# Moving the end of the wide steps, the decay broadcasts and the output stores in a gated-attention plus feed-forward kernel

## Chip, cores and metric

The kernel runs on one core of a Trainium2 chip. The metric is the device time of one execution in microseconds (us). Before the change the median of three runs is 555.83 us (551.5 to 556.11).

## What is computed

For 4 batches and 8 heads of width 40, a recurrence over 768 positions keeps a 40x40 matrix `C`, a vector `n` and a running maximum `m` for each head:

```
m_new = max(f + m, i);  f_stab = exp(f + m - m_new);  i_stab = exp(i - m_new)
C = f_stab * C + i_stab * v k^T;   n = f_stab * n + i_stab * k
y = sigmoid(o) * (C q) / max(|n.q|, 1)
```

The 3072 tokens of 320 features that come out go through a feed-forward layer: `h = x @ w_in` (320x2048), `g = softplus(h)`, `out = g @ w_out` (2048x320). All is float32.

## The kernel before, in words

The recurrence is worked out in chunks of 128 positions: one **step** `s` is one batch and one chunk with all 8 heads, 24 steps in all. Three steps (`g` = 0, 1, 2) make a **tile** of 384 tokens, and there are 8 tiles `t`. The feed-forward layer of a tile is `products()` (L881): for each of 16 slices of `w_in`, 8 matmuls into `hp` (L929), and two slices later 9 matmuls into `po` (L900). These 17 matmuls per slice, 272 per tile, are the **products**, and their running count `n` is the clock by which all other work is placed: after each product `tick(n)` (L865) runs every generator whose place has come. A place only fixes the order of instructions on each engine and on each DMA queue; an instruction then runs when its semaphores allow it, so a queue that has nothing to wait for runs ahead of the products.

Each value of the layer is kept as a high and a low part: `gh` and `ab` on ScalarE (ACT, L806 and L808), `gl` on GpSimd (POOL, L811). `hp` has three buffers, and the `po` products run two slices behind, so these three have some slices' time.

The steps of tile `t` are placed in the products of tile `t`-1. The six tiles from 2 on are **wide** (feature-major). A wide step has a base, in products, and its parts stand at offsets from that base (L257 to L260, `wide_step` L760): its load (L345: six copies of q and k between buffers, sometimes three of a parked state, and the values `vt`, all issued by SyncE, SP) at -48 (or -45 for g = 0); the broadcast read of the decays `fb` (`decays`, L404, SP) at -22; the two scans that make `pw` of them (L413, VectorE, DVE) at 4, then `gw` (L434) and on POOL `vw` (L440); scores `sp` at 6 and 14; the state update `cp` on TensorE (PE, L461), which reads `vw`, at 31; the copies of the new state `cn` (L472, L473, SP) at 53; the products with the old state `iq` at 50 and 62, each followed by a DVE product into `y` (L540); the values `yq` (L548) at 68. Then `y` is turned round through DRAM by DMAs that ACT issues: written at 79 (`yd`, L560), read back at 107 (`read_wide` L562: `yx`, and last the normalizer `nw`, L568). `finish_wide` (L570: four DVE instructions, the first on `nw`) stands at 119 plus a distance `d`, and `end_wide` (L578) at 139 plus `d`: a DVE product, a copy on ACT three products later and a DVE subtraction (L586) three products after that give `X`, the input of the tile's products. `d` is NEAR = 18 for tile 2 and AWAY = 44 for the later ones (L789). The bases of a tile's three steps are some 91 products apart; for g = 2 of tile t > 2 the base is 272t - 200.

The products of tile `t` begin at count 272t - 18. There `products` (L915) first runs all that is queued until the tile's three steps are emitted.

`prepare(t)` (L266) loads q and k of a tile (`loq`, `lok`), splits them on ACT (`hiq`, `hik`) and POOL; the load copies from these. `wide_gates` (L327) loads the output gates of three tiles at a time into `eg` (SP) at `GP`, and applies the sigmoid on ACT 30 products later. When a tile's `po` is complete, `result` (L943) copies it to `ob`, two of three parts on ACT and one on DVE, and stores it four products later through SP. The first two tiles use another, plain form (`plain_step`, L712).

Of the kernel before, what the change touches and what calls it, by code (L numbers as in the profile page):

```python
# [17 lines left out]
NG = 3  # L18
# [14 lines left out]
WIDE = 2  # L33
# [6 lines left out]
def mlstm_moe_kernel(  # L40
# [10 lines left out]
    nc = tc.nc  # L51
# [194 lines left out]
    def weights_out(u):  # L246
# [9 lines left out]

    (W_LOAD, W_FB, W_SCAN, W_CN, W_CS, W_VW, W_SP0, W_SP1, W_Y, W_CP, W_CD,  # L257
     W_IQ0, W_IQ1, W_VI, W_YQ, W_YD, W_RD, W_NM, W_FIN) = (
        -48, -22, 4, 19, -6, 4, 6, 14, 17, 31, 47, 50, 62, 38, 68, 79, 107, 119, 139,
    )  # L260
    N_LOAD, N_FB, N_SCAN, N_CN, N_VW, N_SIG, N_SP0, N_SP1, N_CP, N_CD, N_IP, N_VI, N_YP, N_X, N_XP = (
        -35, -22, 25, 5, 8, 18, 11, 27, 46, 46, 45, 46, 56, 72, 68,
# [76 lines left out]
        yield GL  # L339

    GL = 30
    GP = [150, 1088]
    eg = {}

    def load(z):  # L345
        t, n, gs = z.t, z.n, slice(z.g * D, (z.g + 1) * D)
        if t < PLAIN:

            k = 128 if z.s < 3 else D
            room, tags = (p1, ("loq", "lok")) if z.s == 2 else (p2, ("qst", "kst"))  # L350
            z.qst = room.tile([k, H, L], F32, tag=tags[0], name=f"qst{n}")
            z.kst = room.tile([k, H, L], F32, tag=tags[1], name=f"kst{n}")
            if k > D:
                with tc.issue_after(eye.ins):
                    (nc.gpsimd if z.s == 2 else nc.vector).memset(z.qst, 0.0)
                    nc.gpsimd.memset(z.kst, 0.0)
            nc.sync.dma_start(z.qst[0:D], qk[t, 0, gs])
            nc.sync.dma_start(z.kst[0:D], qk[t, 1, gs])
        else:
            (qh, ql), (kh, kl) = parts[t]  # L360
            z.qst = p2.tile([D3, H, L], F32R, tag="qst", name=f"qst{n}")
            z.kst = p2.tile([D3, H, L], F32R, tag="kst", name=f"kst{n}")
            for r, (a, e) in enumerate(((qh, kh), (qh, kl), (ql, kh))):
                nc.sync.dma_start(z.qst[r * D : (r + 1) * D].bitcast(F32), a[gs].bitcast(F32))
                nc.sync.dma_start(z.kst[r * D : (r + 1) * D].bitcast(F32), e[gs].bitcast(F32))
        if t > 0:
            z.old = None
            if z.c > 0 and not stays(z.b, z.c - 1):
                z.old = p2.tile([D3, H, E2], F32, tag="cn", name=f"pk{n}")
                for r in range(3 if t >= PLAIN else 1):  # L370
                    nc.sync.dma_start(z.old[r * D : (r + 1) * D], park[z.b])
        if z.s != NG:
            load_values(z)
# [16 lines left out]
    def decays(z):  # L390

        z.fbs = []
        h0 = z.b * H
        for i in range(2):
            if z.s < 2:
                fb = ps_h.tile([128, HG, L], F32, tag="hp", name=f"fb{z.n}_{i}")
                for j in range(HG):
                    h = h0 + i * HG + j
                    nc.tensor.matmul(
                        fb[:, j, :], ident[:, h : h + 1].broadcast_to([128, 128]), fg0, start=True, stop=True  # L400
                    )
            else:
                fb = p2.tile([128, HG, L], F32, tag="fb", name=f"fb{z.n}_{i}")
                nc.sync.dma_start(fb, fz_d[z.c, h0 + i * HG : h0 + (i + 1) * HG, :].partition_broadcast(128))  # L404
            z.fbs.append(fb)

    def decay(z):

        z.pws = []
        for i, fb in enumerate(z.fbs):  # L410
            pw = p2.tile([128, HG, L], F32, tag="pw", bufs=4, name=f"pw{z.n}_{i}")
            flat = "p h t -> p (h t)"
            nc.vector.tensor_tensor_scan(  # L413
                pw.rearrange(flat), fb.rearrange(flat), ident4.rearrange(flat), 0.0, ALU.mult, ALU.add
            )
            z.pws.append(pw)
# [19 lines left out]
    def state_values(z):  # L436

        z.vw = work(z, p1, "vw", [128, H, E], "vw", p1, ("vw", "vi", "yy")[z.s % NG])
        v1 = z.v1.rearrange("p (h e) -> p h e", e=E)
        nc.gpsimd.tensor_tensor(z.vw, v1, z.gw.broadcast_to([128, H, E]), op=ALU.mult)  # L440
# [22 lines left out]
    def new_state(z):  # L463
        s, cn = z.s, z.cn
        if z.c > 0:
            nc.vector.tensor_tensor(cn[0:D, :, 0:E], cn[0:D, :, 0:E], z.cp, op=ALU.add)
        else:
            nc.scalar.copy(cn[0:D, :, 0:E], z.cp)
        yield
        if stays(z.b, z.c):  # L470
            if ORDER.index((z.b, z.c + 1)) >= PLAIN * NG:
                nc.sync.dma_start(cn[D : 2 * D], cn[0:D])  # L472
                nc.sync.dma_start(cn[2 * D : D3], cn[0:D])  # L473
            Cst[z.b] = cn
        else:
            nc.sync.dma_start(park[z.b], cn[0:D])
        yield
# [64 lines left out]
    def values_wide(z):  # L542

        yq = ps_a.tile([PP + EP, HG, L], F32, tag="pa", name=f"yq{z.n}")
        for h in range(H):
            p, i = divmod(h, 2)
            e0, e1 = i * PP, PP + i * EP
            nc.tensor.matmul(  # L548
                yq[e0:e1, p, :], z.via[:, h * E : h * E + e1 - e0], z.pws[h // HG][:, h % HG, :], start=True, stop=True
            )  # L550
        yield YQD
        if z.c > 0:
            nc.vector.tensor_tensor(z.y, yq, z.y, op=ALU.add)  # L553
        else:
            nc.vector.tensor_copy(z.y, yq)
        yield "write"
        z.yd = dpool.tile([EP * H, L], F32, tag="yd", bufs=2, name=f"yd{z.n}")
        rows = z.yd.rearrange("(d p i) t -> i d p t", p=HG, i=2)
        for i in range(2):
            nc.scalar.dma_start(rows[i], z.y[i * PP : i * PP + EP])  # L560
# [199 lines left out]
    def wide_step(z):  # L760
        yield W_LOAD if z.g else -45
        load(z)
        yield W_FB
        decays(z)
        yield W_SCAN
        decay(z)
        last = z.c == NC - 1
        yw = values_wide(z)

        def y():  # L770
            for r in yw:
                if r == "write":
                    return
                yield r

        c = new_state(z)
        ev = [(W_Y, lambda: load_decays(z))]
        if not last:
            ev += [(W_CN, lambda: old_state(z)), (W_VW, lambda: last_decays(z)), (W_VW, lambda: state_values(z))]
        if z.c > 0:  # L780
            ev += [(W_CS, lambda: stack(z))]
        ev += [(W_SP0, lambda: scores(z, 0)), (W_SP1, lambda: scores(z, 1))]
        if not last:
            ev += [(W_CP, lambda: state(z)), (W_CP + 6, lambda: next(c)), (W_CD + 6, lambda: next(c))]
        if z.c > 0:
            ev += [(W_IQ0, lambda: inter_wide(z, 0)), (W_IQ1, lambda: inter_wide(z, 1))]
        ev += [(W_VI, lambda: gate_values(z)), (W_YQ, y), (W_YD, lambda: next(yw, None)), (W_RD, lambda: read_wide(z))]

        d = AWAY if z.t > WIDE else NEAR  # L789
        ev += [(W_NM + d, lambda: finish_wide(z)), (W_FIN + d, lambda: end_wide(z))]  # L790
        ev.sort(key=lambda e: e[0])
        for w, f in ev:
            yield w
            r = f()
            if hasattr(r, "__next__"):
                yield from rel(r)

    GV = 5
    AWAY, NEAR = 44, 18

    def activation(t, f, hp, put):
        n = f"{t}_{f}"
# [140 lines left out]
    def result(t, j, po):  # L943
        yield 1
        if j < 2:
            ob = p2.tile([128, DM], F32, tag="ob", name=f"ob{t}_{j}")
        else:
            ob = p1.tile([128, DM], F32, tag="x", name=f"ob{t}_{j}")
        (nc.scalar.copy if "ADA"[j] == "A" else nc.vector.tensor_copy)(ob, po)
        yield 4  # L950
        b, c = ORDER[t * NG + j]
        r0 = b * S + c * L
        nc.sync.dma_start(out[r0 : r0 + 128, :], ob)

    ended = set()

# [7 lines left out]
    with in_order():  # L964
        for k, (u, i) in enumerate(tensors[AHEAD:]):
            if k < 2:
                at = (-8, -2)[k]
            else:
                at = (17 - 2 * 34, 33 - 34)[i] + 34 * u
            start(convert(u, i), at)  # L970
        start(first_states(), 0)
        LEAD, TS = 174, 16 * 17
        EARLIER = 26
        for s in range(NG, NS):
            z = Step(s)
            if z.wide:
                base = TS * z.t - LEAD - EARLIER * (z.t > WIDE) - TS * (NG - 1 - z.g) // NG
                if z.g == 0:
                    start(prepare(z.t), base - 106)
            else:  # L980
                base = [21, 72, 135][s - NG]
            start(whole(z), base)
        start(wide_gates(range(WIDE, WIDE + 3)), GP[0])
        start(wide_gates(range(WIDE + 3, NT)), GP[1])
        zs = first_tile()
        products()
# [37 lines left out]
```

## Time and profile before

| | |
|---|---|
| median of three runs | 555.83 us |
| the profiled execution | 557.21 us, of which the span of the page is 555.2 us |
| mean granted TensorE clock | 0.926 of full speed |
| busy: PE, DVE, POOL, ACT | 491.1, 299.9, 295.8, 197.5 us |
| DMA | 80.63 MB, mean 145 GB/s |

The rows further down are in us from the start of the span. A row of the timeline has the start, the length, the engine (SPq and ACTq are the queues in which SP and ACT issue DMAs) and the line, what is written and read, how many instructions are merged, and in brackets how long the engine sat idle before it and what ended that. PE can be busy at either of two clocks: granted 1.00 is 2.4 GHz, 0.50 is 1.2 GHz.

### The profile page before, as it was taken

What the parts mean: (1) busy time and instruction counts of PE and PEld (TensorE: products, weight loads), DVE (VectorE), ACT (ScalarE), POOL (GpSimd) and SP (SyncE); (2) the same over time, 40 slices, a digit from 0 to 9 for tenths busy, and PEclk for the clock granted to TensorE, in tenths of its full rate; (3) what the DMA queues carried; (4) which work ended last, traced back from release to release, by engine and by line L of the source; (5) the groups of instructions that cost most, each with busy time, mean ns of one, the idle gap of its engine ahead of it and who ended that gap; (6) DMA issues with size and microseconds to landing.
All of it is one profiled execution on the core that took longest, in us unless ns stands there. A gap on an engine that the chain in (4) does not pass through costs nothing.

```text
span 555.2 us, 9173 instructions
## 1 busy us (share of the span) xinstructions
PE 491.1 (88%) x3368; PEld 464.0 (84%) x3368; DVE 299.9 (54%) x433; ACT 197.5 (36%) x401; POOL 295.8 (53%) x324
## 2 busy tenths in 40 slices
PE   7478788889997979898979979799898879999997
PEld 7467678788997979787979979798888879999997
DVE  7776885987637354476254464467354563551001
ACT  2436434563432222423323317343223322333332
POOL 4248786997627543565327543484527643533320
PEclk9859778879998979999898979899899999999999
DMA  7746775935486515674375764765275734311001
GB/s 202 208 145 190 209 212 182 270 120 141 144 204 193 160 34 155 190 193 124 97 199 159 195 181 128 193 178 167 75 196 150 187 86 127 107 35 36 1 1 35
DMA packets 66142, 80.63 MB, mean 145 GB/s; under 512 B 8034, under 2 KB 47122, under 8 KB 66098
## 3 DMA queue, kind: packets, MB, share of 16 engines
q1 hardware_dynamic: 48242, 71.79, 45.5%
q10 hardware_dynamic: 17856, 8.26, 5.7%
q8 instruction: 26, 0.43, 0.3%
q14 instruction: 18, 0.15, 0.1%
HBM read 52.41 MB, written 8.30 MB: 109 GB/s over the span
## 4 chain that ended last, share of the span: by engine, by line
PE 46%; DMA 13%; POOL 12%; DVE 11%; issue 10%; SPq 4%; ACT 3%; ACTq 0%; POOLq 0%; DVEq 0%
PE hp L929 19%; PE po L900 19%; DVE pw L413 3%; DMA qst<-loq 3%; PE yq L548 3%; PE cp L461 2%; POOL gl L811 2%; DMA cn<-cn 2%; POOL loq L283 2%; DMA fb<-fz_d 2%; DMA lok<-in_qk 1%; POOL wol L252 1%; POOL cs L301 1%; POOL vw L440 1%; DVE y L553 1%
## 5 line engine op out<-in xcount | busy, mean ns | idle before, releaser
L811 POOL TENSOR_TENSOR gl<-ab,gh 128x384 fp32r<-128x384 f32 x123 | 135.8, 1106 | 154.0 <-ACT ab L808 144.4
L929 PE MATMUL hp<-X,wih 128*128 128x384 f32 x768 | 192.4, 354 | 17.3 <-DVE X L586 14.8
L929 PEld LDWEIGHTS hp<-X,wih 128*128 128x128 f32 x768 | 139.4, 198 | 22.1 <-DVE X L586 16.7
L806 ACT ACTIVATE gh<-hp 128x384 fp32r<-128x384 f32 x128 | 63.0, 492 | 265.5 <-PE hp L929 209.5
L900 PE MATMUL po<-wol,gh 128*128 128x320 f32 x384 | 86.8, 327 | 4.4 <-POOL wol L252 4.4
L900 PE MATMUL po<-woh,gl 128*128 128x320 f32 x384 | 86.2, 323 | 1.9 <-POOL gl L811 1.9
L900 PE MATMUL po<-woh,gh 128*128 128x320 f32 x384 | 87.3, 326 | 0.6 <-ACT gh L806 0.6
L413 DVE TENSOR_TENSOR_SCAN pw<-fb,ident 128x512 f32<-128x512 f32 x48 | 67.3, 1436 | 33.6 <-DMA fb<-fz_d 31.9
L900 PEld LDWEIGHTS po<-wol,gh 128*128 128x128 f32 x384 | 65.8, 200 | 6.7 <-POOL wol L252 5.5
L929 PE MATMUL hp<-X,wil 128*128 128x384 f32 x256 | 70.8, 357 | 0.0
L900 PEld LDWEIGHTS po<-woh,gh 128*128 128x128 f32 x384 | 68.5, 199 | 2.6 <-ACT gh L806 1.6
L900 PEld LDWEIGHTS po<-woh,gl 128*128 128x128 f32 x384 | 65.2, 198 | 3.2 <-POOL gl L811 2.9
L808 ACT ACTIVATE ab<-hp 128x384 f32<-128x384 f32 x128 | 62.4, 487 | 0.9 <-POOL vi L422 0.9
L540 DVE TENSOR_TENSOR y<-iq,y 41x512 f32<-41x512 f32 x36 | 24.6, 683 | 67.5 <-PE iq L537 65.9
L929 PEld LDWEIGHTS hp<-X,wil 128*128 128x128 f32 x256 | 48.4, 200 | 1.0 <-issue 0.9
L486 DVE TENSOR_TENSOR pw<-sp,pw 128x512 f32<-128x512 f32 x48 | 31.5, 681 | 18.9 <-PE sp L484 18.8
L484 PEld LDWEIGHTS sp<-qst,kst 120*128 120x128 f32 (+2 forms) x240 | 36.0, 212 | 6.3 <-issue 2.5
L484 PE MATMUL sp<-qst,kst 120*128 120x128 f32 (+2 forms) x240 | 36.8, 290 | 4.2 <-DVE X L598 2.2
L440 POOL TENSOR_TENSOR vw<-vt,gw 128x328 f32<-128x328 f32 x19 | 18.2, 960 | 29.7 <-DVE gw L434 28.3
L301 POOL TENSOR_TENSOR cs<-cn,cs 120x336 fp32r<-120x336 f32 x15 | 18.8, 1256 | 18.6 <-ACT cs L300 15.9
L461 PEld LDWEIGHTS cp<-vw,vt 128*40 128x40 f32 x304 | 14.1, 124 | 17.4 <-POOL vw L440 14.8
L461 PE MATMUL cp<-vw,vt 128*40 128x41 f32 x304 | 16.2, 210 | 12.5 <-POOL vw L440 12.5
(124 smaller groups left out, 536.1 us busy)
## 6 DMA issues: line engine op xcount, KB each, us to landing
fb<-fz_d SPq DMA_DIRECT2D x44, 256.0 KB
vt<-in_vko SPq DMA_DIRECT2D x23, 324.0 KB
qst<-hiq SPq DMA_DIRECT2D x36, 160.0 KB
kst<-hik SPq DMA_DIRECT2D x36, 160.0 KB
wo<-in_w_out SPq DMA_DIRECT2D x8, 640.0 KB
wr<-in_w_in SPq DMA_DIRECT2D x8, 512.0 KB
out<-ob SPq DMA_DIRECT2D x24, 160.0 KB
eg<-in_oT SPq DMA_DIRECT2D x18, 192.0 KB
```

The costliest lines, as they stand in the source:

```text
L301: nc.gpsimd.tensor_tensor(z.cs, z.old, z.cs, op=ALU.subtract)
L413: nc.vector.tensor_tensor_scan(pw.rearrange(flat), fb.rearrange(flat), ident4.rearrange(flat), 0.0, ALU.mult, ALU.add)
L440: nc.gpsimd.tensor_tensor(z.vw, v1, z.gw.broadcast_to([128, H, E]), op=ALU.mult)
L461: nc.tensor.matmul(z.cp[:, h, :], z.kt[:, h * D : (h + 1) * D], z.vw[:, h, :], start=True, stop=True)
L484: nc.tensor.matmul(sp[:, j, :], z.kst[:, h, :], z.qst[:, h, :], start=True, stop=True)
L486: nc.vector.tensor_tensor(z.pws[i], sp, z.pws[i], op=ALU.mult)
L540: nc.vector.tensor_tensor(y, iq, y, op=ALU.mult)
L806: nc.scalar.activation(gh, hp, AF.Softplus)
L808: nc.scalar.activation(ab, hp, AF.Softplus)
L811: (nc.vector if u >= NT * NF - GV else nc.gpsimd).tensor_tensor(gl, ab, gh, op=ALU.subtract)
L900: nc.tensor.matmul(po[j], a[:, j * 128 : (j + 1) * 128], w[:, f, :], start=(f == 0 and left[j] == 2), stop=(last and left[j] == 0),)
L929: nc.tensor.matmul(hp, a, r, start=(i == 0), stop=(i == len(seq) - 1))
```

## The change

It sets `d` to 18 for all wide steps, so that those of tiles 3 to 7 are finished 26 products earlier; it begins the steps of tile 2 six products earlier. It sets the place of `decays` to -52; as that lies ahead of the load's own place, and `resume` (L856) never goes back, the broadcast is issued directly behind the load. It issues the output stores from ACT, twelve products after the copy instead of four. The second group of output gates is loaded 32 products earlier, and two plain steps begin 2 and 7 products earlier.

```diff
-        -48, -22, 4, 19, -6, 4, 6, 14, 17, 31, 47, 50, 62, 38, 68, 79, 107, 119, 139,
+        -48, -52, 4, 19, -6, 4, 6, 14, 17, 31, 47, 50, 62, 38, 68, 79, 107, 119, 139,
...
-    GP = [150, 1088]
+    GP = [150, 1056]
...
-        d = AWAY if z.t > WIDE else NEAR
+        d = AWAY
...
-    AWAY, NEAR = 44, 18
+    AWAY = 18
...
-        yield 4
+        yield 12
         b, c = ORDER[t * NG + j]
         r0 = b * S + c * L
-        nc.sync.dma_start(out[r0 : r0 + 128, :], ob)
+        nc.scalar.dma_start(out[r0 : r0 + 128, :], ob)
...
-        EARLIER = 26
+        EARLIER = [6, 26]
...
-                base = TS * z.t - LEAD - EARLIER * (z.t > WIDE) - TS * (NG - 1 - z.g) // NG
+                base = TS * z.t - LEAD - EARLIER[z.t > WIDE] - TS * (NG - 1 - z.g) // NG
...
-                base = [21, 72, 135][s - NG]
+                base = [21, 70, 128][s - NG]
```

## Rows read from the trace of the kernel before

**Rows 1.** The page, busy time of each engine over the whole span.
```profile
PE 491.1 (88%) x3368; PEld 464.0 (84%) x3368; DVE 299.9 (54%) x433; ACT 197.5 (36%) x401; POOL 295.8 (53%) x324
```

**Rows 2.** Waits of PE, 130 to 506.5 us: total, times, longest.
```profile
PE hp L929 <- DVE X L586: 14.8, 6, 2.9
PE cp L461 <- POOL vw L440: 11.3, 6, 2.9
PE yq L548 <- DVE y L540: 2.1, 1, 2.1
```

**Rows 3.** Timeline of DVE ahead of the first product of tile 4.
```profile
322.08 0.56 DVE L582 TENSOR_TENSOR eg<-yx,eg 128x384 f32<-128x384 f32 x1
322.56 3.10 DVE L413 TENSOR_TENSOR_SCAN pw<-fb,ident 128x512 f32<-128x512 f32 x2
...
326.36 0.55 DVE L586 TENSOR_TENSOR X<-eg,X 128x384 fp32r<-128x384 f32 x1
```

**Rows 4.** Waits of DVE, 201 to 480 us.
```profile
DVE pw L413 <- DMA fb<-fz_d: 23.9, 12, 4.3
```

**Rows 5.** Timeline of DVE and of PE, step 14 (tile 4, g = 2).
```profile
286.92 1.23 DVE L413 TENSOR_TENSOR_SCAN pw<-fb,ident 128x512 f32<-128x512 f32 x1 [4.27 <-DMA fb<-fz_d]
...
291.08 0.78 PE L461 MATMUL cp<-vw,vt 128*40 128x41 f32 x16 [2.95 <-POOL vw L440]
```

**Rows 6.** Timeline of SP's queue: around the load of step 14, then of step 17.
```profile
256.21 0.60 SPq L325 DMA_DIRECT2D y<-fc_d  x1
271.51 1.31 SPq L953 DMA_DIRECT2D out<-ob  x3
...
281.25 0.37 SPq L388 DMA_DIRECT2D vt<-in_vko  x1
281.66 1.10 SPq L404 DMA_DIRECT2D fb<-fz_d  x2
282.86 0.39 SPq L272 DMA_DIRECT2D loq<-in_qk  x1
...
344.73 1.15 SPq L472 DMA_DIRECT2D cn<-cn  x1
...
346.71 1.10 SPq L404 DMA_DIRECT2D fb<-fz_d  x2
```

**Rows 7.** Stretches: us; PE, PEld, DVE, ACT, POOL busy (instructions); granted clock; DMA share; GB/s.
```profile
176.00:179.40 3.40, 3.12 (x21) 2.82 (x22) 2.82 (x5) 0.52 (x2) 1.24 (x2) 0.50 0.95 285
...
264.80:268.20 3.40, 3.40 (x15) 3.40 (x14) 0.14 (x1) 0.87 (x2) 1.00 (x1) 0.50 0.16 46
...
327.00:333.00 6.00, 6.00 (x22) 6.00 (x23) 1.20 (x2) 0.87 (x2) 2.24 (x4) 0.50 0.63 180
...
511.30:543.70 32.40, 32.40 (x206) 32.40 (x205) 1.52 (x4) 10.90 (x25) 9.88 (x10) 1.00 0.05 16
```

**Rows 8.** Timeline, read-back of step 7 (tile 2, near distance).
```profile
169.62 0.62 ACTq L568 DMA_DIRECT2D nw<-yd  x1
...
171.88 0.33 DVE L572 TENSOR_SCALAR nm<-nw 128x128 f32<-128x128 f32 x1 [2.74 <-DMA nw<-yd]
...
176.28 1.95 PE L548 MATMUL yq<-pw,vi 128*64 128x128 f32 x16 [2.09 <-DVE y L540]
```

**Rows 9.** Timeline, read-backs of step 13 (g = 1) and step 14 (g = 2).
```profile
290.68 1.05 ACT L277 CAST hiq<-loq 120x1024 fp32r<-120x1024 f32 x1 [5.98 <-DMA loq<-in_qk]
...
292.46 0.37 ACTq L564 DMA_DIRECT2D yx<-yd  x1
...
312.72 0.55 ACTq L568 DMA_DIRECT2D nw<-yd  x1
...
314.64 0.41 PE L537 MATMUL iq<-qst,cs 120*41 120x128 f32 x4
```

**Rows 10.** Timeline of ACT: the sigmoid of three tiles' gates.
```profile
339.90 3.27 ACT L337 ACTIVATE eg<-eg 128x1152 f32<-128x1152 f32 x3
```

**Rows 11.** Output stores: all of L953 (ns min/median/max; first and last start).
```profile
L953 SPq DMA_DIRECT2D out<-ob x24: 332/360/1133, 142.9 to 552.4; - x24
```

## The prediction

> **What bounds the kernel now.** I read the page first: PE is busy for 491.1 us of the span of 555.2, every other engine for 300 or less [rows 1]. So time can only be won where PE waits or runs slowly. The waits of PE, cut to the stretch in which the wide steps stand, say where: 14.8 us in six waits for `X`, the input of a tile, five of them at some 2.9 us; 11.3 us in six waits of `cp` for `vw`; and one of 2.1 us of `yq` for a DVE product [rows 2].
>
> The timeline of DVE shows what the wait for `X` is made of. At the start of tile 4 `end_wide` begins at 322.08; the product is done half a microsecond later, but the subtraction that ends `X` starts at 326.36, because two scans of a later step stand between them on DVE and take 3.10 us [rows 3]. The order written by the places makes it so: for g = 2 the end stands at count 272t - 17, its subtraction at 272t - 11, and the scans of the step two further on, whose base is 272t - 18, at 272t - 14, between the two.
>
> The waits of `cp` begin further back. DVE stands idle for 23.9 us in 12 waits of a scan for `fb` [rows 4]. In step 14 the scan starts 4.27 us late, and `cp`, which needs scan, `gw` and `vw`, keeps PE waiting for 2.95 us [rows 5]. `fb` was late because SP was: its queue issued nothing from 256.8 to 271.5 us, standing at the stores of a finished tile, whose results did not exist yet; only then came the load of step 14, ten DMAs, and behind it `fb` at 281.66 [rows 6].
>
> Each wait of this size is paid for again. Behind the wait of `X` at tile 4 PE runs at 0.50, which is 1.2 GHz, for 6.0 us; behind the one at tile 3 for 3.4 us [rows 7]. There are seven such stretches between 200 and 460 us: behind five waits for `X` and two of the longest `cp` waits, two of some 6 us and five of 3.4. The wait of only 2.1 us at 176 has one too.
>
> **The change, part by part.** The profiled execution took 557.2 us, 1.4 more than the median of the runs; the sum is made against it.
>
> *The end, 26 products earlier.* For g = 2 the end now stands at 272t - 43 and the last subtraction at 272t - 37: 19 products ahead of the tile's first product, and ahead of the scans at 272t - 14. At 0.157 us a product (206 in 32.4 us [rows 7]) that is 3.0 us; the copy and the subtraction still to come take about one. For tile 2 the distance stays and the base moves six back: the subtraction at 272t - 17 then precedes the scans at 272t - 14. All six waits go: -14.8 us. What comes next on DVE, the scans, is no later than before.
>
> *The output stores on ACT.* Each costs ACT a median of 0.36 us of issuing [rows 11], 1.1 us per tile, twelve products behind the copy, so it should find its data. ACT had 3.3 us taken from it at once at 339.9 us, by the sigmoid of three tiles [rows 10], and PE's waits for ACT are too small to stand among the first three [rows 2]; I cost the issue at nothing. If that cover is gone, it is 1.1 us in six tiles, 7 us at most. SP, freed of its 14.7 us stand, can issue the load of g = 2 as soon as its buffers are free, many microseconds sooner, and `fb` and `loq` behind it. At the end of the kernel two stores now stand before the last one on ACT: 2 x 0.36 = +0.7 us.
>
> *`fb` directly behind the load.* In step 14 it already stood right behind `vt` (281.25, then 281.66), so the new place alone moves nothing there; in step 17 it overtakes the `cn` copies, 2.0 us [rows 6]. For g = 2 the two edits together bring `fb` forward by more than the 4.3 us that the scan lacked; the four waits of this kind are the larger part of the 11.3. For g = 0 there is no stand at the stores, and the load waits for the POOL split; the 2.0 us must do, for the other two waits. I take -10 of the -11.3; the bounds are -2 and -11.3. Behind `fb` on SP now stand the `cn` copies, 1.1 to 2 us later where the order decides; ACT reads them for `stack`, 56 products before PE needs that. I cost it at nothing; uncovered, it would hold `gh` back, which nothing on this page prices higher than the DVE wait below.
>
> *The clock.* Five stretches of 3.4 us and two of 6 at half speed lose half their length: 8.5 + 6.0 = 14.5 us. With the waits gone these go.
>
> *The new wait.* `finish_wide` now stands 30 products behind the read-back instead of 56, and DVE works in order: if `nw` has not landed, the `iq` products of the next step stand behind it, and `yq` on PE waits for those. Tile 2 had this distance, and shows the price: `nw` issued at 169.62, landed 2.26 us later, DVE idle for 2.74, PE idle for 2.09 [rows 8] and then 3.4 us at half speed [rows 7]: 2.1 + 1.7 = 3.8 us. It struck one of that tile's three steps. In the later tiles, a g = 1 step is late because ACT stands for 5.98 us waiting for `loq`, and only then issues the read-back, at 292.46 [rows 9]; with SP freed, `loq` (282.86 [rows 6]) comes with the earlier load and this goes. For g = 2, `nw` of step 14 is issued at 312.72 and by the 2.26 us lands at 315.0; the new place is four products before the next step's `iq` at 314.64 [rows 9], at 314.0: 1.0 us late, and more where a shorter `cp` wait pulls the place forward. I take three of the four g = 2 steps of tiles 3 to 6 as paying 3.8: +11.4. Bounds: none, or all eight g = 1 and g = 2 steps of these tiles, +30.4.
>
> *The rest.* The six products at tile 2, the plain steps and the gates at 1056 reorder work of stages where DVE and POOL set the pace; the trace has no row for either order. I take 0, with 3 us to either side.
>
> **Sum.** 557.2 - 14.8 - 10 - 14.5 + 11.4 + 0.7 = 530.0; less the 1.4 by which this execution stands above the median, 529.
>
> **Rivals.** *A: the broadcast comes no sooner.* If the load of g = 2 does not run ahead (a buffer that is freed later than I think, POOL's split), then the `cp` waits stay with their two stretches at half speed: 530.0 + 10 + 3.4 - 1.4 = 542. For it: in step 14 the new place of `fb` is the old one. Against it: the 14.7 us stand of SP, which ends with the stores and with nothing else. The Trainium skill ("DMA: Bandwidth & Descriptors", section "Issuing engines are not separate DMA queues") says that issuing from several engines saves only the sequencer's time to initiate a DMA. By that rule the stores' move is worth 1.3 us per tile and this rival holds; the trace speaks against it, since what SP loses here is a wait on a semaphore, not issuing time. Chance 0.15.
>
> *B: the read-back is late in all eight g = 1 and g = 2 steps of tiles 3 to 6*, because ACT still stands at `loq`: +30.4 in place of +11.4, 548. For it: the 5.98 us stand; against it: SP's earlier `loq`. Chance 0.18, split between faster and no change.
>
> *C: slower.* The broadcast of 512 KB, now directly behind a load of 1.3 MB, fills the DMA engines just as the previous step's read-back is on its way, so that every g = 1 and g = 2 step, and g = 0 too, has DVE waiting for `nw`. Twelve steps at 3.8 are 45.6 against a full gain of 557.2 - 517.3 = 39.9: 517.3 + 45.6 - 1.4 = 562. It decides from eleven steps at that price on, or from fewer if each is longer. Against it: of the three steps with this distance in tile 2, `yq` waited in one [rows 2]. Chance 0.09.
>
> **How the numbers follow.** The forecast has 0.58. Its own range reaches from no new wait and all of the `cp` waits, 557.2 - 14.8 - 11.3 - 14.5 + 0.7 - 1.4 = 516, to 542. With A and most of B inside, the range is 516 to 549. About 1% is what a measurement here can tell from no change, 550.3 to 561.4 us. Faster: 0.58 + 0.15 + 0.07 of B = 0.80; the same: 0.11, the rest of B; slower: 0.09.
>
> **What would show it.** In the profile after, PE's wait for `X` of L586 is gone and the subtraction of g = 2 stands before the scans; SP has no long stand at L953 and the load of g = 2 follows the `y` decays at once; scans wait for `fb` for less than 5 us in all, and `cp` hardly for `vw`; ACT no longer stands at `hiq`; DVE's wait at L572 for `nw` has grown, in the g = 2 steps above all; the mean granted clock rises from 0.926. I am wrong if PE's waits for `yq` or for `gh` come to 20 us or more, or if `X` is still late because ACT's copy stands behind something.

## The result, and the profile after

The changed kernel takes 545.6 us, median of four runs (544.9 to 550.4), beside 553.7 of four runs of the kernel before (the 555.83 us known ahead is the median of three of them); the ratio is 0.9873, with a 95% interval of 0.983 to 0.9916. It is faster by 1.3%, where 4.8% were forecast (529 us against 555.83): inside the range of 516 to 549, with about a quarter of the gain. The profiled execution took 546.2 us, its span is 544.5.

What the change was to take away is gone. These are PE's waits from 145 to 510 us, in the profile after (total, times, longest):

```profile
PE yq L548 <- DVE y L540: 14.5, 5, 3.2
PE po L900 <- ACT ob L949: 6.8, 2, 4.4
PE hp L929 <- ACT X L584: 1.4, 1, 1.4
PE po L900 <- POOL wol L252: 0.5, 1, 0.5
PE hp L929 <- DVE X L586: 0.3, 1, 0.3
```

The waits for `X` have fallen from 14.8 us to 1.7 (of which 1.4, at tile 2, are for ACT's copy), those of `cp` from 11.3 to nothing [rows 2]; in their place stand 14.5 us of `yq` and 6.8 of `po`. No scan waits for `fb` [rows 4]: in SP's queue the broadcast of step 14 goes out at 263.05, 18.6 us sooner than before [rows 6]:

```profile
256.05 0.71 SPq L365 DMA_DIRECT2D kst<-lok  x1
...
262.58 0.37 SPq L388 DMA_DIRECT2D vt<-in_vko  x1
263.05 0.84 SPq L404 DMA_DIRECT2D fb<-fz_d  x2
263.94 0.43 SPq L272 DMA_DIRECT2D loq<-in_qk  x1
```

What `yq` waits for is seen on DVE. These are rows of its timeline in step 13 (tile 4, g = 1) and of POOL's beside them:

```profile
289.83 1.89 DVE L572 TENSOR_SCALAR nm<-nw 128x128 f32<-128x128 f32 x1
291.75 5.12 DVE L573 TENSOR_TENSOR nm<-nw,nm 128x128 f32<-128x128 f32 x1
296.90 0.95 DVE L574 RECIPROCAL nm<-nm 128x128 f32<-128x128 f32 x1
...
298.37 1.39 DVE L540 TENSOR_TENSOR y<-iq,y 41x512 f32<-41x512 f32 x2
```

```profile
290.26 1.29 POOL L283 TENSOR_TENSOR loq<-loq,hiq 120x512 fp32r<-120x512 f32 x1
291.49 0.11 POOL L422 MEMSET vi<- 128x7 f32 x1
291.55 0.76 POOL L425 TENSOR_TENSOR vi<-vt,gT 128x328 f32<-128x328 f32 x1
292.27 1.00 POOL L811 TENSOR_TENSOR gl<-ab,gh 128x384 fp32r<-128x384 f32 x1
293.24 2.52 POOL L283 TENSOR_TENSOR lok<-lok,hik 120x512 fp32r<-120x512 f32 x2
295.73 0.99 POOL L811 TENSOR_TENSOR gl<-ab,gh 128x384 fp32r<-128x384 f32 x1
```

DVE is not idle here, it is busy: an instruction that takes 0.29 us elsewhere (the median of the 18) takes 5.12. It ends at 296.87, just as POOL's unbroken row of instructions from 291.49 ends at 296.72. `L572` ahead of it, which reads one tensor, takes 1.89 us in place of 0.22. The four instructions of that finish take 8.6 us from start to end; in step 14 of the kernel before they took 2.1 (319.92 to 322.05). The same happens in all four g = 1 steps of tiles 3 to 6. `yq` then waits 3.15 to 3.17 us each time.

The read-back for g = 0 is late in another way. These are rows of tile 4's first step on ACT, DVE and PE:

```profile
267.79 0.55 ACTq L568 DMA_DIRECT2D nw<-yd  x1
...
269.14 0.76 ACT L949 COPY ob<-po 128x320 f32<-128x320 f32 x2
```

```profile
274.83 0.44 DVE L572 TENSOR_SCALAR nm<-nw 128x128 f32<-128x128 f32 x1 [8.90 <-DMA nw<-yd]
```

```profile
269.62 0.74 PE L900 MATMUL po<-woh,gh 128*128 128x320 f32 x3 [2.39 <-ACT ob L949]
```

`nw` lands some 7 us after its issue, where 2.26 was the row of before [rows 8]. The early load, the broadcast, `loq` and `lok` had gone out on SP from 253 to 265 us, and these are the two stretches from the issue to the first use of `nw`, of tile 4 in the kernel after, then of rows 8 in the kernel before (columns as in [rows 7]):

```profile
267.80:274.80 7.00, 5.18 (x25) 5.03 (x26) 0.00 (x0) 2.67 (x7) 2.37 (x4) 0.76 0.97 247
```

```profile
169.60:171.90 2.30, 1.56 (x13) 1.33 (x11) 0.02 (x1) 1.61 (x4) 2.30 (x3) 1.00 0.41 129
```

The DMA engines were busy for 0.97 of the one and 0.41 of the other. In `u_out` below, which puts the stores back on SP and so holds these loads back, DVE does not stand for `nw` at this place. And ACT, whose issues of the read-back stretch to 268, copies a finished tile too late for PE.

The first tiles have lost time as well. Product 254, the first of tile 1 (counted along L929 and L900), starts at 143.1 us instead of 136.1; from it to the end of the last product the time fell from 415.7 to 397.5 us. PE's longest new wait there, and the POOL instructions ahead of it:

```profile
103.98 1.33 PE L929 MATMUL hp<-X,wih 128*128 128x384 f32 x3 [6.08 <-POOL wih L243]
```

```profile
100.46 1.72 POOL L283 TENSOR_TENSOR lok<-lok,hik 120x512 fp32r<-120x512 f32 x1 [6.94 <-DMA kst<-lok]
102.14 1.26 POOL L241 TENSOR_TENSOR wil<-sgi,wih 128x512 fp32r<-128x512 f32 x1
103.47 0.98 POOL L243 TENSOR_TENSOR wih<-sgi,wih 64x128 fp32r<-64x128 f32 x2
```

POOL stood for 6.94 us at a split of tile 2, waiting for the DMA that reads the same buffer, and the weights that PE needed stood behind it. In the kernel before they stood ahead of that split:

```profile
95.87 1.62 POOL L241 TENSOR_TENSOR wil<-sgi,wih 128x512 fp32r<-128x512 f32 x1
97.58 1.70 POOL L243 TENSOR_TENSOR wih<-sgi,wih 64x128 fp32r<-64x128 f32 x2
99.36 2.27 POOL L283 TENSOR_TENSOR lok<-lok,hik 120x512 fp32r<-120x512 f32 x1
```

### The profile page after: what moved, and what is told of

The parts are those of the page before. It is cut to its first block, busy times and chain, and to the rows that moved or that the text cites. A ratio compares the mean times of both kernels' runs of the same rounds, so it can differ in the third digit from the quotient of the medians.

```text
span 544.5 us, 9170 instructions
## 1 busy us (share of the span) xinstructions
PE 479.7 (88%) x3368; PEld 456.1 (84%) x3368; DVE 316.3 (58%) x433; ACT 197.1 (36%) x401; POOL 282.2 (52%) x324
## 4 chain that ended last, share of the span: by engine, by line
PE 53%; DMA 16%; DVE 12%; issue 7%; ACT 4%; POOL 3%; SPq 2%; ACTq 1%; DVEq 0%; POOLq 0%
PE hp L929 23%; PE po L900 22%; DMA nw<-yd 4%; DMA qst<-in_qk 3%; PE yq L548 3%; DVE nm L573 3%; PE sp L484 2%; DMA yd<-y 2%; DVE nm L572 2%; DMA fb<-fz_d 2%; PE cp L461 2%; DVE sgi L203 1%; DVE nm L574 1%; DMA og<-in_vko 1%; POOL gl L811 1%
## 5 line engine op out<-in xcount | busy, mean ns | idle before, releaser
L929 PE MATMUL hp<-X,wih 128*128 128x384 f32 x768 | 188.2, 350 | 10.9 <-POOL wih L243 8.6
L929 PEld LDWEIGHTS hp<-X,wih 128*128 128x128 f32 x768 | 138.5, 196 | 14.1 <-POOL wih L243 9.2
L900 PE MATMUL po<-woh,gh 128*128 128x320 f32 x384 | 84.2, 319 | 10.1 <-ACT ob L949 6.8
L900 PE MATMUL po<-wol,gh 128*128 128x320 f32 x384 | 83.6, 319 | 5.4 <-POOL wol L252 5.4
L900 PE MATMUL po<-woh,gl 128*128 128x320 f32 x384 | 85.8, 320 | 0.0
L900 PEld LDWEIGHTS po<-woh,gh 128*128 128x128 f32 x384 | 67.2, 195 | 11.6 <-ACT ob L949 7.4
L929 PE MATMUL hp<-X,wil 128*128 128x384 f32 x256 | 71.0, 355 | 0.0
L900 PEld LDWEIGHTS po<-wol,gh 128*128 128x128 f32 x384 | 63.1, 193 | 7.4 <-POOL wol L252 6.1
L900 PEld LDWEIGHTS po<-woh,gl 128*128 128x128 f32 x384 | 64.1, 194 | 0.4 <-issue 0.3
L413 DVE TENSOR_TENSOR_SCAN pw<-fb,ident 128x512 f32<-128x512 f32 x48 | 61.9, 1331 | 2.5 <-PE fb L399 2.5
L929 PEld LDWEIGHTS hp<-X,wil 128*128 128x128 f32 x256 | 47.3, 196 | 1.8 <-issue 1.6
L484 PEld LDWEIGHTS sp<-qst,kst 120*128 120x128 f32 (+2 forms) x240 | 33.3, 197 | 5.4 <-DVE X L598 3.0
L540 DVE TENSOR_TENSOR y<-iq,y 41x512 f32<-41x512 f32 x36 | 24.5, 681 | 22.3 <-PE iq L537 20.5
L572 DVE TENSOR_SCALAR nm<-nw 128x128 f32<-128x128 f32 x18 | 15.4, 854 | 38.0 <-DMA nw<-yd 37.9
L548 PE MATMUL yq<-pw,vi 128*64 128x128 f32 (+1 forms) x288 | 22.1, 302 | 14.6 <-DVE y L540 14.5
L548 PEld LDWEIGHTS yq<-pw,vi 128*64 128x64 f32 (+1 forms) x288 | 17.4, 143 | 18.7 <-issue 18.1
L573 DVE TENSOR_TENSOR nm<-nw,nm 128x128 f32<-128x128 f32 x18 | 27.0, 1499 | 0.6
```

The lines of the kernel that those rows point to most:

```text
L413: nc.vector.tensor_tensor_scan(pw.rearrange(flat), fb.rearrange(flat), ident4.rearrange(flat), 0.0, ALU.mult, ALU.add)
L484: nc.tensor.matmul(sp[:, j, :], z.kst[:, h, :], z.qst[:, h, :], start=True, stop=True)
L540: nc.vector.tensor_tensor(y, iq, y, op=ALU.mult)
L548: nc.tensor.matmul(yq[e0:e1, p, :], z.via[:, h * E : h * E + e1 - e0], z.pws[h // HG][:, h % HG, :], start=True, stop=True)
L572: nc.vector.tensor_scalar(nm, z.nq, -1.0, 1.0, op0=ALU.mult, op1=ALU.max)
L573: nc.vector.tensor_tensor(nm, z.nq, nm, op=ALU.max)
```

## The experiments

Each was timed beside the kernel before in five rounds; a ratio is the time over that of the kernel before. Small differences hold only where the intervals do not meet. Three theories say where the rest of the gain went. P: DVE's instruction at L573, moved by 26 products, has to let a row of POOL's instructions pass. G: the gates' sigmoid at its new place makes ACT late for the finished tile. F: the front places (tile 2 six products earlier, the plain steps) cost what the first tiles lost. Against them stands rival B of the prediction, the read-back that has not landed.

**The parts alone**, each put into the kernel before.

The stores on ACT, `p_out`:

```diff
-        yield 4
+        yield 12
-        nc.sync.dma_start(out[r0 : r0 + 128, :], ob)
+        nc.scalar.dma_start(out[r0 : r0 + 128, :], ob)
```

> The kernel before with one part: the output stores on ACT, twelve products behind the copy. By my prediction SP then loads g = 2 early, the four cp waits of g = 2 go (8.8 us with 3.4 us of half speed) and ACT no longer stands at loq: 538 to 545. By rival A (only issuing time is saved): 551 to 554. If the early loads crowd the read-back, as the profile after suggests, the gain is eaten where nw is needed, but here it is needed 26 products later, so it should not show.

Measured: 538.7 us, ratio 0.9733 (0.9691 to 0.9776). This one part brings twice what the whole change does. PE's waits from 200 to 510 us:

```profile
PE hp L929 <- DVE X L586: 10.1, 5, 2.9
PE hp L929 <- ACT X L584: 2.1, 1, 2.1
```

No `cp` wait is left, with the broadcast at its old place; the waits for `X` are untouched (a further one of 2.7 us, at tile 2, ends at 197 us, just ahead of this view). Rival A falls.

The end 26 products earlier, `p_end` (`AWAY, NEAR = 18, 18`; the gates' place stays, with the consequence told at `u_gp`):

> The kernel before with one part: the distance 18 for the steps of tiles 3 to 7 too (the second group of gates stays at 1088, so the first step that uses it, the first of tile 5, is finished with gates to which the sigmoid has not been applied). Theory P: PE's waits for X at tiles 3 to 7 go (11.9 us and some 8 us of half speed), the cp waits stay, and yq waits come: some 3 us in each of four g = 1 steps from DVE held beside POOL's splits, and more for the read-back, since ACT still stands at loq; 540 to 549. Theory R, the read-back alone: DVE waits at its first instruction, not at its second, and the time is 545 to 555.

Measured: 552.9 us, ratio 0.9955 (0.9916 to 0.9994), next to nothing. From 200 to 510 us:

```profile
PE yq L548 <- DVE y L540: 12.9, 5, 3.5
PE cp L461 <- POOL vw L440: 6.8, 4, 2.2
PE hp L929 <- DVE X L586: 2.9, 1, 2.9
```

The waits for `X` at tiles 3 to 7 are gone (the 2.9 us are tile 2's), and 12.9 us of `yq` have come. Without the stores' move it is the read-back that is late, in g = 1 by 4.8 to 6.3 us at DVE's first instruction, as rival B had it; the second one takes at most 1.3 us. So theory P, which expected the long second instruction here too, was wrong for this kernel.

The broadcast behind the load, `p_fb` (`W_FB` = -52):

> The kernel before with one part: the decays' broadcast directly behind the load. By my prediction's part this alone overtakes only the cn copies: the two cp waits of g = 0 go (2.6 us), those of g = 2 become some 2 us shorter where cn stood in front, X waits stay: 546 to 552 against 553. If the broadcast in front of the cn copies makes ACT late: 553 to 557.

Measured: 554.3 us, ratio 1.0019 (0.9984 to 1.0055): no gain. The scans' waits for `fb` fell (from 23.9 us to 12.9), but `cp` still waits 9.1 us in all.

**One part undone**, in the changed kernel.

The stores back on SP, `u_out` (`nc.sync.dma_start(out...)`):

> The changed kernel with the output stores back on SP (twelve products behind the copy). Theory S (SP's stand at the stores is what kept fb late): SP stands again, g = 2 loads late, cp waits come back, and the time rises from 545.6 to 552 to 560. Theory C (the early loads crowd the DMA engines and cost as much as they bring): PE's wait for ob at tile 4 and DVE's 8.9 us for the read-back there go, and the time stays within 542 to 549.

Measured: 560.6 us, ratio 1.0111 (1.006 to 1.0162). SP stands at L953 again, and with the stores on SP the rest of the change is slower than the kernel before. (Here the stores stand twelve products behind the copy, not four, so it is not quite the change without this part.)

The middle steps at the old distance, `u_g1`:

```diff
-        d = AWAY
+        d = 44 if z.t > WIDE and z.g == 1 else AWAY
```

> The changed kernel, with the middle step (g = 1) of tiles 3 to 7 alone finished at the old distance of 44. Theory P (DVE and POOL hold each other up): in the changed kernel the second instruction of finish_wide takes 5.12 us instead of 0.29 in four g = 1 steps, at the place where POOL splits the next tile's q and k, and yq then waits 3.15 to 3.17 us each time; with g = 1 finished 26 products later these four waits (12.6 us) and three stretches at half speed (some 5 us) go, and the time falls from 545.6 to 528 to 533. Theory R (the read-back has not landed, as I predicted): DVE did not stand idle for the read-back in those four steps, so a later finish brings at most 2 us, 543 to 546.

Measured: 538.6 us, ratio 0.9748 (0.9697 to 0.9798). All instructions of L573 (ns min/median/max), then PE's waits of `yq`:

```profile
L573 DVE TENSOR_TENSOR nm<-nw,nm x18: 291/293/1266, 155.4 to 481.0; 128x128 f32<-128x128 f32 x18
```

```profile
PE yq L548 <- DVE y L540: 9.7, 4, 3.2
```

The 5.12 us are gone, and 7 us of time with them. The rest of the expected gain did not come: `nw` is late for g = 2 in tiles 3 and 5, by 5.7 and 6.4 us (in the changed kernel by nothing and 5.2), and PE waits 2.7 us behind each.

Two of POOL's four splits left out, `u_split`:

```diff
-        for hi, lo in parts[t]:
+        for hi, lo in parts[t][: 1 if t > WIDE else 2]:
```

> The changed kernel without the two POOL subtractions that split k in tiles 3 to 7 (so k's low part stays the whole of k: it leaves out two of a tile's four splits). Theory P: the finish of g = 1 stays where it is, but POOL's work beside it is shorter by two times 1.28 us, so the second instruction of finish_wide falls from 5.12 us to some 2.5, and yq's wait from 3.2 to under 1: 531 to 537. Theory R, and any theory in which only the order on DVE counts: the 5.12 us stay, 543 to 546.

Measured: 538.9 us, ratio 0.9767 (0.9717 to 0.9818). The finish of g = 1 stands where the change put it, and the same instruction of step 13 now takes

```profile
292.42 1.68 DVE L573 TENSOR_TENSOR nm<-nw,nm 128x128 f32<-128x128 f32 x1
```

which ends at 294.1, where POOL's own row of work, two splits shorter, ends too (293.96; POOL is idle from there to its next instruction):

```profile
295.23 1.34 POOL L811 TENSOR_TENSOR gl<-ab,gh 128x384 fp32r<-128x384 f32 x1 [1.27 <-ACT ab L808]
```

It does so in all four g = 1 steps, and no `yq` wait is left there. Less work on POOL, nothing moved on DVE: theory P holds for these waits. The time lies 2 us above the range expected.

The broadcast at its old place, `u_fb` (`W_FB` = -22):

> The changed kernel with the decays' broadcast at its old place, -22. If the broadcast directly behind the load crowds the read-back (rival C of the prediction): DVE's waits for nw fall from 37.9 us, and the time falls to 536 to 542. If it does not matter beside the early loads: 543 to 548. If it is what keeps cp from waiting: cp waits come back, 550 to 556.

Measured: 545.4 us, ratio 0.9847 (0.9797 to 0.9898): no different from the changed kernel. It shows that the hold is not L573's alone. In its step 13 the instruction ahead, which reads one tensor, has it, and ends 0.1 us behind POOL's row (297.52):

```profile
290.65 6.96 DVE L572 TENSOR_SCALAR nm<-nw 128x128 f32<-128x128 f32 x1
```

There L573 takes 0.29.

The gates at the old place, `u_gp` (`GP = [150, 1088]`; the first step of tile 5 is then finished with gates to which no sigmoid has been applied):

> The changed kernel with the second group of output gates loaded at 1088 again. In the changed kernel the copies of a finished tile's results on ACT stand behind the sigmoid of three tiles, and po waits 4.36 us for them at 335 us, with a stretch at half speed behind. If the earlier gates did that (theory G): this one wait goes, 539 to 541. If ACT is late there anyway, because of the read-back (theory R): 544 to 547.

Measured: 549.5 us, ratio 0.9937 (0.9894 to 0.998). Of the two waits of `po` for `ob` one is left (2.1 us), so the other was the sigmoid's, as theory G had it; but the time did not fall, and lies outside both ranges expected. The profiled execution took 554.4 us, 5 more than the median, so that its other waits are no measure. It settles nothing about the time.

The front places undone, `u_front` (`EARLIER` 0 for tile 2, plain steps at 21, 72, 135):

> The changed kernel with the old places of the plain steps (21, 72, 135) and of tile 2 (none earlier). The changed kernel reaches product 254 at 143.1 us, the kernel before at 136.1, with new waits of PE for converted weights. If the earlier places did that (theory F), those 7 us come back: 538 to 540, and product 254 near 136. If it is the stores on ACT, or the broadcast in front of weight loads on SP (theory Q), the time stays at 544 to 547. Tile 2 may lose 1 to 2 us, its last subtraction again behind two scans.

Measured: 550.7 us, ratio 0.9953 (0.9917 to 0.9989). Product 254 starts at 136.6, as theory F had it, but the time did not follow: it is above both ranges expected, and above the changed kernel, by intervals that just do not meet. From 130 us on `yq` waits 18.1 us in six waits, and `X` at tile 2 for 2.9 again.

**Towards a better version.**

Stores and end together, `v_end_out` (`p_out` with `AWAY` = 18 and the gates at 1056):

> The kernel before with two parts, the stores on ACT and the distance of 18 everywhere (gates at 1056, which that distance needs); broadcasts, plain steps and tile 2 as before. If the end's move is what takes back the stores' gain (538.7 alone): 542 to 549, with DVE's 5.12 us beside POOL's splits. If the broadcast in front, or the front places, are what takes it back: 526 to 536.

Measured: 539.2 us, ratio 0.9741 (0.9692 to 0.9789), against 0.9733 for the stores alone. The end's move brings nothing beside the stores either, and takes nothing back; the time lies between the two ranges expected. This kernel differs from the changed one only in the broadcast's place and the front places, so these two together cost 1.3%. With `u_front` and `u_fb` it makes a square:

| | front places old | front places new |
|---|---|---|
| broadcast at -22 | `v_end_out` 0.9741 | `u_fb` 0.9847 |
| broadcast at -52 | `u_front` 0.9953 | changed kernel 0.9873 |

With the broadcast at its old place the front places cost 1.1%; with the front places old, the broadcast directly behind the load costs 2.1%; neither pair of intervals meets. The two do not add up, so undoing one alone could not show what either costs. What the broadcast delays is not shown: the profiled execution of `v_end_out` took 546.2 us, 7 more than the median, and its waits cannot be set beside those of `u_front`.

g = 0 and g = 1 both at 44, `v_g2` (`d = AWAY if z.t == WIDE or z.g == 2 else 44` in the changed kernel):

> The changed kernel with g = 0 and g = 1 of tiles 3 to 7 at the old distance of 44, only g = 2 at 18. Against the changed kernel (545.6) and the one with g = 1 alone at 44 (538.6): if the first step's read-back (8.9 us of DVE at tile 4, yq waiting behind) still costs there (theory C), 530 to 536; if only g = 1 mattered (theory P alone), 537 to 541.

Measured: 534.9 us, ratio 0.9673 (0.9625 to 0.972): lower than `u_g1`'s 0.9748, with intervals that overlap. The two distances together bring 2%; the share of g = 0 in that is likely, not shown.

Stores, and only the end of g = 2 at 30, `v_p30`, on `p_out`:

```diff
-        d = AWAY if z.t > WIDE else NEAR
+        d = NEAR if z.t == WIDE else 30 if z.g == 2 else AWAY
```

> The kernel before with the stores on ACT, and of the end's move only what the order of X needs: the last step of each of tiles 3 to 7 (g = 2) at a distance of 30, so that its last subtraction stands ten products ahead of the later scans; g = 0 and g = 1 stay at 44, the broadcasts and all other places as before. The stores alone gave 538.7 with 12.8 us of waits for X left, four tiles of them in reach (11 us, with some 8 us of half speed). If the order on DVE is all that X needs (theory O): these go and nothing comes, 521 to 530. If any earlier finish is paid back in waits for the read-back (theory R): 534 to 541.

Measured: 525.0 us, ratio 0.9488 (0.944 to 0.9535), the fastest. From 200 to 510 us PE has one long wait, one of 2.3 us, and little else:

```profile
PE hp L929 <- ACT X L584: 4.1, 1, 4.1
PE po L900 <- ACT ob L949: 2.3, 1, 2.3
PE po L900 <- ACT gh L806: 0.3, 1, 0.3
```

No `yq` wait is among them, and no wait of L586; the one of tile 2, 2.9 us as before, ends at 197 us, ahead of this view. DVE shows the order that did it, ahead of tile 4:

```profile
307.98 0.56 DVE L586 TENSOR_TENSOR X<-eg,X 128x384 fp32r<-128x384 f32 x1 [1.40 <-ACT X L584]
308.45 3.11 DVE L413 TENSOR_TENSOR_SCAN pw<-fb,ident 128x512 f32<-128x512 f32 x2
```

In [rows 3] the scans stood first.

Four variants of `v_p30`. g = 2 at 38, `w_d38`:

> The kernel of v_p30 with g = 2 at 38 in place of 30: X's last subtraction stands two products ahead of the later scans, one product behind the place where PE needs it. If only its order before the scans counts: 524 to 527. If X must also be done before PE comes to it: some 1 to 2 us of wait at five tiles, 529 to 535.

Measured: 532.2 us, ratio 0.9653 (0.96 to 0.9705). PE waits four times, 7.9 us, for ACT's copy into `X`, where `v_p30` has one such wait of 4.1: the order before the scans is not enough, `X` has to be done too.

The plain steps at the new places, `w_plain`, and tile 2 six products earlier, `w_t2`:

> The kernel of v_p30 (stores on ACT, the last step of tiles 3 to 7 at 30; 525.0 us) with the new places of the two plain steps. The changed kernel reaches product 254 at 143 us, the one with the old front places at 136.6. If the plain places are what makes PE wait for converted weights (theory F1): product 254 at 141 to 145 and 530 to 533. If they are not: 524 to 526.

> The kernel of v_p30 with the steps of tile 2 six products earlier. If the earlier load of tile 2 is what delays POOL's split and the weights (theory F2): product 254 at 141 to 145, and 527 to 532, the wait for X at tile 2 (2.9 us with 3 us of half speed) gone. If it is not: that wait goes at no price, 518 to 522.

Measured: 532.8 us, ratio 0.9649 (0.9589 to 0.9709), and 528.9 us, ratio 0.9618 (0.9562 to 0.9673). Product 254 starts at 138.7 and at 143.4, against 135.4 in `v_p30`. Both front places cost time. The plain steps cost 7.8 us, of which only 3.3 are there by product 254; where the rest goes was not followed up. Tile 2's six products bring the wait for `wih` (from 60 to 145 us), and at tile 2 a wait of some 3 us for ACT's copy into `X` takes the place of the one for L586:

```profile
PE hp L929 <- POOL wih L243: 5.2, 1, 5.2
```

The broadcast behind the load, `w_fb`:

> The kernel of v_p30 with the broadcast directly behind the load. With the stores on ACT no scan waits for fb any more, so there is nothing to win: 524 to 526 if it is only placed differently; 529 to 535 if, being in front of the cn copies and of weight loads, it makes the read-back or the first tiles later (rival C of the prediction, in small).

Measured: 528.3 us, ratio 0.9596 (0.9549 to 0.9643); in the profile the `yq` wait of tile 2, at 157 us, is 3.8 us in place of 2.1. It is of no use, and costs 1%, by intervals that just do not meet.

## Why the prediction was wrong

*What bounds the kernel*: right. The waits for `X` and of `cp` went as read, by the mechanisms read; `v_p30`, which takes only these two causes away, and `X` not at tile 2, gains 5.1%. The sum without its new wait comes to 517 us, 7%, and was somewhat too high. One reading was short: the two long stretches at half speed last 6.8 us (326.2 to 333.0 us at tile 4), not 6.0, so that the seven are worth 15.4 us and not 14.5.

*The stores on ACT with the broadcast*: right in size (10 us and two stretches at half speed, 13.4 us; the stores alone measured 553 times 0.0267, 14.8 us), wrong in naming the broadcast's place as a half of it: the stores do it alone, and that place brought nothing in `p_fb` and cost time in `w_fb` and `u_front`. The sentence of the Trainium skill ("DMA: Bandwidth & Descriptors", section "Issuing engines are not separate DMA queues") that issuing from several engines saves only issuing time did not decide, as argued: what SP lost was its stand behind a semaphore.

*The new wait* is the step that failed. The sum has the end's move bring 14.5 us: 14.8 of waits for `X` and 11.1 of half speed, less 11.4 for a read-back not yet landed, in three g = 2 steps at 3.8 us. By the parts the new waits eat all that the end's move brings, since that move measured 0.9955 alone, and 0.9741 against 0.9733 beside the stores. Three things were missing.

First, a collision that I did not look for: the finish of g = 1 at 137 products falls where POOL does the next tile's splits, at 109 to 151 of that step, and L573 ends only when POOL's row does; `u_g1` and `u_split` both take it away and gain over 1%. The kernel before had the sign in it, L573 at up to 1.28 us in the g = 1 steps of tiles 2 to 6, and I read only the idle time of DVE, not its busy time:

```profile
172.24 1.27 DVE L573 TENSOR_TENSOR nm<-nw,nm 128x128 f32<-128x128 f32 x1
```

This is step 7, the very step that priced the term [rows 8]: up to 1 us of its 2.09 was this hold and not the read-back. The Trainium skill has this ("SBUF — State Buffer", section "Who interferes with whom"): a DVE instruction with two SBUF inputs contends with a GpSimd instruction that reads SBUF, and the one that starts later is blocked. The trace agrees for L573: 5.12 us beside POOL's unbroken row, 1.68 when that is two splits shorter, 0.29 without it. L572, held for 6.96 us in `u_fb`, has one input and is not the case of that sentence.

Second, I priced the landing of `nw` by a row of 2.26 us, among the shortest; with SP running ahead it took some 7 us in the first step of tile 4. DVE's waits for `nw` grew from 7.2 us to 37.9, and some 17 of these are in g = 0 steps, which neither the term nor its bounds had, and of the rivals only C. Third, ACT's copies of a finished tile, 6.8 us of `po` waits, which I did not have.

*The clock*: from 140 to 510 us the stretches at half speed fell only from 34.1 us in all to 20.5, since five of the six new waits of over 2 us have one beside them. The wait of 3.15 us that ends at 299.19 us has none (columns as in [rows 7]):

```profile
299.20:303.00 3.80, 3.80 (x33) 3.61 (x34) 3.77 (x6) 1.39 (x3) 1.01 (x1) 1.00 0.56 169
```

*The rest, 0 with 3 us to either side*: too small. The front places cost 7 us by product 254, most of it from tile 2's six products; together with the broadcast's place, costed at nothing, they make the 1.3% between `v_end_out` and the changed kernel. So the parts, put in one after the other, make up the result: the stores -2.7%, the end's move 0.1, the rest 1.3, in all -1.3%. Why the front places and the broadcast's place cost less together than the broadcast's place alone stays open.

*Rival B* (the read-back late in eight steps, 548) came nearest in time, but its cause, ACT at `loq`, is not what happened: with SP freed ACT did not stand there. It is what happened in `p_end`. The sign set for being wrong, 20 us of waits of `yq` or `gh`, did not come either: `yq` waits 14.5 us.

## What to carry to other kernels

When a step on an in-order engine is moved closer to its input, look at everything that runs on the neighbouring engines at the new place, and not only at whether the input is there: an instruction can be held while it counts as busy. Move as little as the order needs: in `v_p30` the last subtraction stands eleven products ahead of the blocking scans (272t - 25 against 272t - 14), for one step in three, and that was worth more than 26 products for all steps. A store that waits at the head of a load queue costs the wait, not its issue; here it was worth moving first, and alone.

## What was not expected of the hardware

A DVE maximum of 128x128 (L573) that elsewhere takes 0.29 us took 5.12 us beside a row of POOL instructions without a gap, and ended within 0.2 us of the last of them; in `u_fb` the instruction ahead of it, with one input, took 6.96 us in the same way. A read-back that ACT issued landed some 7 us after its issue, against 2.26 us in a quieter place; SP had issued nearly 3 MB of loads in the 14 us before (the loads from 253 to 265 us, by the KB of the issue rows), and the DMA engines were busy for 0.97 of these 7 us. A wait of PE of 2.1 us had a stretch at half speed behind it [rows 7] [rows 8], one of 3.15 us had none.
